# New constants for an order planner: engine durations by kind of instruction, and smaller margins between engines, in a gated mix of two attentions

## The chip, the cores and the metric

The kernel runs on one core of a Trainium2 chip. Its time is the device time of one execution in microseconds. The core's engines are TensorE (PE in the profile, with PEld for its weight loads), VectorE (DVE), ScalarE (ACT), GpSimd (POOL) and SyncE (SP, which issues DMAs here).

## The reference

Two attentions over the same x (2048 rows, 512 columns, bf16) are mixed by a gate per row. A is full attention with 32 heads of 16 columns; B looks at 8 positions back from each row, two apart.

```
g = sigmoid((x * gate_w).sum(-1))
A: q,k,v = split(x @ A_wqkv); p = softmax(q k^T / 4) over all 2048 keys; a = (p v) @ A_wo
B: q,k,v = split(x @ B_wqkv); keys and values at s, s-2, ..., s-14 (masked below 0);
   b = (softmax of 8 logits, times the 8 values) @ B_wo
out = g * a + (1 - g) * b
```

## The kernel before

**Attention A.** The work is cut into 32 periods, each one group of 4 heads and one block of 512 queries. A period has 64 units; a unit is one head, one tile of 128 keys and the 512 queries. For a unit PE computes scores into PSUM (a *ring fill*, tile `ring`), ACT takes the exponential into `pT`, and PE multiplies with the values into `acc` (`pvA`). Two ring buffers alternate, one of 3 units and one of 2, so ACT's instructions are 1536 and 1024 columns wide in turn, and a pair of them makes 5 units. Since ACT is not to do all of it, some groups of 4 units, called *quads*, are done on DVE: `conv` (`dt<-m_ps`, 128x512, four per quad) makes the bits of an approximate exponential by one multiply and add, `term` (`dt<-dt`, 128x2048, two per quad) makes two shifted copies, and PE sums the three with weighted values (`vd_all`). `start_quad` decides when a quad is begun, from the time that the planner sees left for the period and from what waits on DVE.

At the end of a period DVE transposes `acc` (`accT`), takes reciprocals (`rden`), POOL scales into `ott`, and DVE turns every second one back (`oat`), ready for the output product.

**Attention B.** It runs beside A, in 16 tiles of 128 rows (`b_tile`). PE projects, DVE evacuates into `kvs`, SP stores to a scratch in HBM and loads it again, shifted, as `ksh` and `vsh`. POOL then does all elementwise work of a tile in one chain: products with `ksh` (`prod<-ksh,qb`), tree sums (`prod<-prod`), logits `lg`, the subtraction of the maximum that DVE took (`mx`), after ACT's exponential and DVE's sum (`ssum`) the normalization, products with `vsh`, sums, and the result `obb`. PE transposes obb (`m_ps<-ident,obb`), DVE copies it to `obt`, and PE multiplies with `bwo`.

**Output.** `final` makes, for each 128 rows, the product with `bwo` (DVE evacuates it times 1-g into `fb`) and the product with A_wo (DVE evacuates it times g, plus fb, into `osb`); for the last block of queries the first three quarters of A's product are made ahead and kept as fp32 in `kt_all`.

**What sets the order.** All instructions are recorded first as `Op` objects, each with its engine, a duration in ns, dependencies, buffers to acquire and release, and a due time. The planner (`Sched`) then runs a model of the five engines in the build and writes the instructions out in the order of its start times; each engine executes its own list in that order, and semaphores keep the dependencies. So the durations in the planner are never executed. They decide which instruction is put ahead of which, and how many quads are given to DVE. The parts of the model that matter here are these:

- `est` gives the time at which an op is ready: the end of each dependency, plus the entry of `MARGIN` (line 58) for the pair of engines. An op that follows one on its own engine takes `gap` instead.
- `commit` advances an engine. DVE's `lock` ops and POOL's ops are made to exclude each other, with `HEAD` (line 66) as the part of an instruction that may overlap; `lead` (line 223) is how far the next instruction of an engine may start ahead of the end of the last.
- In `pe_source`, a ring fill is due 480 ns before the time at which ACT is expected to be idle, and line 1121 sums that up from the fills in hand. In `act_source`, line 1205, an exponential's duration is given. With ACT's lead of 127 ns a planned exponential takes 427 ns per unit and 83 ns.

```
act_idle = max(act_idle, f_["vis"]) + len(f_["us"]) * 427.0 + 83.0      # line 1121
op = Op("ACT", None, dur=nu * 426.7 + 210.0, name="exp")                # line 1205
```

- `warm` puts zero matmuls of the full array (`ones_t,zw`, 128x512) in front of an op while the planned share of streaming time in the last 3413 ns is under a threshold.

PE executes its list in order, so whatever PE waits for holds up the ring fills behind it.

Of the kernel before, what the change touches and what calls it, by code (L numbers as in the profile page):

```python
# [57 lines left out]
MARGIN = {("POOL", "DVE"): 2500.0, ("POOL", "PE"): 3000.0, ("DVE", "PE"): 300.0, ("PE", "DVE"): 100.0,  # L58
# [7 lines left out]
HEAD = {"DVE": 130.0, "POOL": 125.0}  # L66
# [51 lines left out]
class Sched:  # L118
# [82 lines left out]
    def commit(self, op, ready):  # L201
# [9 lines left out]
        else:  # L211
            op.start = max(self.t[e], ready)
            op.fin = op.start + op.dur
            if op.lock:
                begun, end = self.pool_op
                if begun <= op.start < end:
                    op.fin = max(op.fin, end - HEAD["DVE"] + op.dur)
                self.lock_end = op.fin
            elif e == "POOL":
                if op.start < self.lock_end:  # L220
                    op.fin = max(op.fin, self.lock_end - HEAD["POOL"] + op.dur)
                self.pool_op = (op.start, op.fin)
            lead = {"DVE": 80.0, "ACT": 127.0, "POOL": 40.0, "SP": 0.0}[e]
# [108 lines left out]
def kernel(  # L332
# [147 lines left out]
    load("x0", x_load(0), 6500.0)  # L480
    load("x1", x_load(1), 10000.0)
# [32 lines left out]
    S_.t["PE"] = 5600.0  # L514
# [5 lines left out]
    def k_proj(i, sc, due, first=False):  # L520
# [26 lines left out]
        p1 = Op("PE", part(0, 2), mms=COL4 * 3, deps=xt_ops[sc] + [ld["wk0" if i == 0 else "wk"]], due=due, acq=[hold], not_before=0.0 if first else due - 5000.0,  # L547
                name="k1")
        p2 = Op("PE", part(2, DC), mms=COL4 * 2, deps=[p1], due=due, name="k2")
        for o in (p1, p2):  # L550
            S_.add(o)
        if first:
            r = S_.add(Op("DVE", red, dur=700.0, deps=[p2], due=due, name="kred"))
            e = S_.add(Op("ACT", evac, dur=650.0, deps=[p2, r], due=due, rel=[hold], name="kev"))
        else:
            e = S_.add(Op("DVE", evac, dur=690.0, deps=[p2], allow=400.0, rel=[hold], name="kev"))
            r = S_.add(Op("DVE", red, dur=800.0, deps=[e], allow=1500.0, name="kred"))
# [5 lines left out]
    def selk(i, reds, due):  # L563
# [4 lines left out]
        selk_ops[i] = S_.add(Op("DVE", s, dur=650.0, deps=reds, due=due, name="selk"))  # L568
# [3 lines left out]
    def v_proj(h0, h1, tb, TB, due):  # L572
# [24 lines left out]
        ops.append(Op("DVE", evac, dur=690.0, allow=400.0, rel=[hold], name="vev"))  # L597
# [20 lines left out]
    def q_proj(c_, i, due):  # L618
# [24 lines left out]
        def evac():  # L643
# [6 lines left out]
               Op("DVE", absq, dur=690.0, allow=300.0, name="qabs"),  # L650
               Op("PE", bound, mms=COL4, due=due, rel=[ha], deps=[selk_ops[i]], name="qb"),
               Op("DVE", evac, dur=690.0, allow=300.0, rel=[hold], name="qev")]
# [46 lines left out]
    def b_tile(t, due):  # L699
# [19 lines left out]
        def store():  # L719
# [4 lines left out]
              Op("DVE", kev, dur=690.0, allow=600.0, rel=[hk], name="bkev")]  # L724
        vv = [Op("PE", pj("v", hv, 0, 2), mms=COL4 * 2, deps=xd + [kv[1]], due=due, acq=[hv], name="bv1"),
              Op("PE", pj("v", hv, 2, 4), mms=COL4 * 2, due=due, name="bv2"),
              Op("DVE", vev, dur=690.0, allow=600.0, deps=[kv[2]], rel=[hv], name="bvev")]
# [6 lines left out]
        def qev():  # L734
# [5 lines left out]
              Op("DVE", qev, dur=690.0, allow=1000.0, rel=[hq], name="bqev")]  # L740
# [35 lines left out]
        def padd(fn, dur, after_last=True, early=False, **kw):  # L776
            late = len(pool) > 17 and not early
            o = Op("POOL", fn, dur=dur, due=float(2 * t + (3 if late else 0)), name="bp", **kw)
            o.gap = 78.0 if after_last else -40.0
# [23 lines left out]
        for hf in range(2):  # L803
            for w_ in range(WH):
                first = w_ == 0
                padd(lmul(hf, w_), 1150.0, after_last=False, acq=([hp[hf]] if first else []) + ([hlg] if first and hf == 0 else []),
                     deps=[lk, qq[-1]] if first and hf == 0 else [])
            padd(ltree(hf, 8, 0, 2), 1255.0)
            padd(ltree(hf, 8, 2, 4), 1255.0, after_last=False)
            padd(ltree(hf, 4, 0, 4), 1255.0)  # L810
            padd(ltree(hf, 2, 0, 4), 612.0)
            padd(ltree(hf, 1, 0, 4), 418.0, rel=[hp[hf]] + ([hks, hqb] if hf else []))
# [32 lines left out]
        s_ = padd(sm_sub, 640.0, early=True, deps=[m_])  # L845
        x_ = S_.add(Op("ACT", sm_exp, dur=490.0, allow=500.0, deps=[s_], name="smexp"))
        d_ = S_.add(Op("DVE", sm_sum, dur=757.0, allow=2500.0, deps=[x_], name="smsum"))
        padd(sm_norm, 640.0, deps=[d_])
# [23 lines left out]
        level = []  # L872
        for w_ in range(W):
            padd(amul(w_, len(level)), 1095.0, after_last=w_ == 0, acq=[hp[2]] if w_ == 0 else [], deps=[lv] if w_ == 0 else [],
                 rel=[hvs, hlg] if w_ == W - 1 else [])
            level.append(0)
            while len(level) > 1 and level[-1] == level[-2] and len(level) + level[-1] < 5 and (level[-1] < 2):
                padd(aadd(len(level) - 2), 1255.0)
                level.pop()
                level[-1] += 1  # L880
        padd(fin1, 1264.0, acq=[hobb], rel=[hp[2]])
# [11 lines left out]
        def fin3():  # L893
# [4 lines left out]
             Op("DVE", fin3, dur=420.0, allow=800.0, rel=[hb], name="bf3")]  # L898
# [10 lines left out]
    def post(c_, i, pv_ops):  # L909
# [27 lines left out]
        def back():  # L937
# [3 lines left out]
        ops = [Op("DVE", turn, dur=720.0, allow=-2000.0, deps=pv_ops, acq=[hT],  # L941
                  rel=[acc_hold[(c_, i)]], name="accT", prompt=True),
               Op("DVE", rec, dur=240.0, allow=a, name="rec"),
               Op("DVE" if last else "POOL", scale, dur=450.0 if last else 640.0, due=-1.0, acq=[] if half else [ho], rel=[hT],
                  name="scale")]
        if half:
            ops.append(Op("DVE", back, dur=710.0, allow=a, acq=[oat_hold[pair]], rel=[ho], name="oatT"))
# [11 lines left out]
    def final(c_, tt, k0, k1, due):  # L959
# [31 lines left out]
        if not tail:  # L991
# [4 lines left out]
            fb = Op("DVE", bev, dur=690.0, allow=600.0, rel=[hold], deps=list(g_done), name="fbev")  # L996
# [15 lines left out]
        ops.append(Op("DVE", evac, dur=700.0, allow=0.0 if tail else 600.0, deps=[fb], rel=[hold] + ([] if tail else [hf]), name="fev"))  # L1012
# [92 lines left out]
    def pe_source(e):  # L1105
# [8 lines left out]
        if us and w < INF:  # L1114
# [3 lines left out]
            if r < INF and S_.slots["pTA" if n == 3 else "pTB"].when() < INF:  # L1118
                act_idle = S_.t["ACT"]
                for f_ in filled:  # L1120
                    act_idle = max(act_idle, f_["vis"]) + len(f_["us"]) * 427.0 + 83.0
# [74 lines left out]
    def act_source(e):  # L1196
# [8 lines left out]
        op = Op("ACT", None, dur=nu * 426.7 + 210.0, name="exp")  # L1205
# [101 lines left out]
    def make_quad(p, t, late):  # L1307
# [7 lines left out]
        for j in range(4):  # L1315
# [21 lines left out]
            a_ = S_.add(Op("DVE", conv, dur=690.0, deps=[f_] + aops[-1:], due=min(S_.now, late - 6000.0) + 300.0 * j - 5000.0, rel=[hold],  # L1337
# [137 lines left out]
```

## Time and profile before

| what | value |
|---|---|
| runs, us | 798.77, 799.01, 799.29, 801.13, 802.75; median 799.29 |
| the profiled execution, us | 801.13 |
| its span, first to last instruction, us | 798.8 |
| mean granted TensorE clock | 0.989 |
| ACT's exponentials (pT) | 656 instructions, 750.7 us busy |
| first pT starts, last one ends, us | 18.87, 788.3 |
| DVE's conversions dt<-m_ps and terms dt<-dt | 408, 269.8 us, and 204, 224.7 us |
| full-array zero matmuls into acc | 143, 50.2 us |
| POOL's first product, last obb ends, us | 56.41, 781.8 |

The profiled execution is one of the five runs. Busy time is the union of an engine's instructions; consecutive exponentials overlap a little, so their mean durations (1497 and 1072 ns for the two widths) add up to more than it. A row of the waits names who waited, for whom, the us in total, how often and the longest. In the timeline's rows stand start, length, engine, line, operation, count, and in brackets the idle time before and what ended it. Nearly all instructions carry line 382, that of the recording helper, so groups are told apart by their tiles.

### The profile page before, as it was taken

The page shows a single profiled execution, that of the slowest core. Times are in us where ns is not written, and L with a number is a line of the kernel's source. Part 1 is how long each engine was busy: PE and PEld are TensorE (multiplying, and loading weights), DVE is VectorE, ACT ScalarE, POOL GpSimd, SP SyncE. Part 2 cuts the span into 40 slices and gives each one's busy share as a digit, 9 for nine tenths or more (in the row PEclk, how much of TensorE's full clock was granted, in tenths as well). Part 3 has the DMA queues.
Part 4 walks back from the last instruction along what each step waited for, and adds up shares of the span by engine and source line. Part 5 has one row for each costly group of instructions (what it writes and reads, how often), then busy time and mean ns, then how long its engine had stood idle before and what let it go on. Part 6 is the DMA issues. An engine that isn't in the chain of part 4 may idle for free.

```text
span 798.8 us, 20306 instructions
## 1 busy us (share of the span) xinstructions
PE 743.6 (93%) x8523; PEld 234.6 (29%) x8523; DVE 679.7 (85%) x1019; ACT 756.9 (95%) x678; POOL 694.6 (87%) x599
## 2 busy tenths in 40 slices
PE   7999999999989999999999999999999999999996
PEld 2332233333222223332222222333322222322222
DVE  2569979888998998979988999898999998797886
ACT  2999999999999999998989999999999999999994
POOL 1028799999999999999989999999999999999991
PEclk9999999999999999999979999999999999999998
DMA  9220321122111211121012121120212212221100
GB/s 201 92 68 14 107 68 54 68 67 54 42 43 38 68 54 67 53 68 54 28 41 67 54 67 54 50 72 2 70 65 80 67 54 68 67 61 41 41 15 34
DMA packets 52074, 47.46 MB, mean 59 GB/s; under 512 B 12048, under 2 KB 49424, under 8 KB 51984
## 3 DMA queue, kind: packets, MB, share of 16 engines
q1 hardware_dynamic: 50400, 45.98, 18.5%
q8 instruction: 66, 1.08, 0.5%
q10 hardware_dynamic: 1584, 0.20, 0.2%
q14 instruction: 24, 0.20, 0.1%
HBM read 37.75 MB, written 6.32 MB: 55 GB/s over the span
## 4 chain that ended last, share of the span: by engine, by line
ACT 39%; PE 26%; DVE 19%; issue 11%; POOL 2%; SPq 1%; DMA 1%; ACTq 0%; DVEq 0%; POOLq 0%
ACT pT L382 39%; DVE dt L382 13%; PE m_ps L382 10%; PE acc L382 9%; PE ring L382 6%; POOL prod L382 2%; SPq L382 1%; DVE accT L382 1%; DVE kt_all L382 1%; DVE absq L382 1%; ACT lg L382 1%; DVE kmax_all L382 1%; DMA xT<-in_A_x_dram 0%; DVE kvs L382 0%; DVE selk_all L382 0%
## 5 line engine op out<-in xcount | busy, mean ns | idle before, releaser
L382 ACT ACTIVATE pT<-ring 128x1536 bf16<-128x1536 f32 (+1 forms) x656 | 750.7, 1284 | 17.6 <-PE ring L382 16.1
L382 PE MATMUL ring<-qt,kt_all 32*128 32x512 bf16 x1640 | 279.0, 384 | 28.7 <-ACT pT L382 25.7
L382 DVE TENSOR_SCALAR dt<-m_ps 128x512 uint16<-128x512 f32 x408 | 269.8, 679 | 42.0 <-PE m_ps L382 33.5
L382 POOL TENSOR_TENSOR prod<-prod 128x512 f32<-128x512 f32 x224 | 294.2, 1319 | 10.7
L382 DVE TENSOR_SCALAR dt<-dt 128x2048 uint16<-128x2048 uint16 x204 | 224.7, 1103 | 1.1 <-PE acc L382 0.4
L382 PEld LDWEIGHTS <-kt_all 32*128 32x128 bf16 (+1 forms) x2304 | 92.1, 91 | 289.6 <-issue 279.1
L382 POOL TENSOR_TENSOR prod<-ksh,qb 128x512 f32<-128x512 bf16 x128 | 160.8, 1284 | 12.5 <-DVE qb L382 5.3
L382 PE MATMUL acc<-pT,vp_all 128*17 128x512 bf16 x1640 | 159.5, 385 | 0.1
L382 POOL TENSOR_TENSOR prod<-vsh,lg 128x512 f32<-128x512 bf16 x128 | 151.7, 1201 | 4.7
L382 PE MATMUL m_ps<-qt,kt_all 32*128 32x512 bf16 x408 | 138.7, 385 | 7.3 <-DVE dt L382 4.5
L382 PEld LDWEIGHTS <-vp_all 128*17 128x17 bf16 x2048 | 47.2, 88 | 109.0 <-issue 100.0
L382 POOL TENSOR_TENSOR ott<-accT,rden 128x256 bf16<-128x256 f32 x31 | 24.5, 790 | 54.1 <-DVE rden L382 54.1
L382 PE MATMUL acc<-ones_t,zw 128*128 128x512 bf16 (+1 forms) x271 | 62.9, 392 | 3.7 <-DVE accT L382 3.7
L382 PE MATMUL acc<-dt,vd_all 128*17 128x512 bf16 x816 | 62.1, 381 | 0.0
L382 PE MATMUL m_ps<-bw,xT 128*32 128x512 bf16 x768 | 55.9, 382 | 1.2 <-DVE kt_all L382 0.4
L382 PEld LDWEIGHTS <-xT 128*32 128x32 bf16 (+1 forms) x1152 | 32.5, 96 | 28.9 <-issue 22.1
L382 PE MATMUL acc<-dt,vp_all 128*17 128x512 bf16 x408 | 40.2, 384 | 0.0
L382 PE MATMUL m_ps<-xT,wkv 128*16 128x512 bf16 x512 | 38.1, 387 | 1.3 <-DMA xT<-in_A_x_dram 1.3
L382 PE MATMUL m_ps<-xT,wq 128*16 128x512 bf16 x496 | 36.4, 380 | 0.0
L382 PEld LDWEIGHTS <-zw 128*32 128x32 bf16 (+1 forms) x401 | 19.4, 94 | 54.6 <-issue 51.2
L382 DVE CAST kvs<-m_ps 128x512 bf16<-128x512 f32 x32 | 21.8, 681 | 9.7 <-PE m_ps L382 9.5
L382 DVE CAST kt_all<-m_ps 128x512 bf16<-128x512 f32 x28 | 19.2, 684 | 11.6 <-PE m_ps L382 11.5
(71 smaller groups left out, 451.0 us busy)
## 6 DMA issues: line engine op xcount, KB each, us to landing
ksh<-kv_scr SPq DMA_DIRECT2D x16, 1024.0 KB, 5.7
vsh<-kv_scr SPq DMA_DIRECT2D x16, 1024.0 KB, 5.4
kv_scr<-kvs SPq DMA_DIRECT2D x16, 256.0 KB, 2.0
out_dram<-osb SPq DMA_DIRECT2D x16, 128.0 KB, 1.7
bw<-in_B_wqkv_dram SPq DMA_DIRECT2D x1, 1536.0 KB, 10.3
wkv<-in_A_wqkv_dram SPq DMA_DIRECT2D x2, 448.0 KB, 5.1
bwo<-in_B_wo_dram SPq DMA_DIRECT2D x1, 512.0 KB, 4.5
woarr<-in_A_wo_dram SPq DMA_DIRECT2D x8, 64.0 KB, 2.3
```

The lines of the kernel that those rows point to most:

```text
L382: return chain_on(key, f(*a, **k))
```

## The change

Only constants of the planner change, and flags that say which op follows its predecessor's result.

- **ACT**: the fixed part of an exponential goes from 210 to 178 (83 to 51 after the lead), in both places.
- **Margins**: POOL to DVE 2500 to 1500, POOL to PE 3000 to 1500, DVE to PE 300 to 200, PE to DVE 100 to 60.
- **POOL**: durations of single ops by some ns (products 1150 to 1149 and 1095 to 1094, tree sums 1255 to 1260, sums 1255 to 1268, `sm_sub` and `sm_norm` 640 to 628, `scale` 640 to 616), the gap after an independent op from -40 to -43, and `after_last` set by what each op really depends on.
- **DVE**: evacuations and conversions 690 to 683, `kred` 800 to 677, `selk` 650 to 446 and now among the lock ops, `fbev` and `fev` 690 and 700 to 745, `smsum` 757 to 791, transposes 720 to 716 and 710 to 707.
- **Lock**: HEAD 130 and 125 to 133 and 137, leads of DVE and POOL 80 and 40 to 83 and 43.
- **Start**: PE's first planned time 5600 to 7800, the landing of x 6500 and 10000 to 8100 and 11500, and the first K projection counted twice as long.

In the order that is built, ACT has 1644 units in 658 instructions where it had 1640 in 656, DVE 101 quads where it had 102, and PE 111 full-array zero matmuls where it had 145. SP issues the same transfers, some in another order.

```
-MARGIN = {("POOL", "DVE"): 2500.0, ("POOL", "PE"): 3000.0, ("DVE", "PE"): 300.0, ("PE", "DVE"): 100.0,
+MARGIN = {("POOL", "DVE"): 1500.0, ("POOL", "PE"): 1500.0, ("DVE", "PE"): 200.0, ("PE", "DVE"): 60.0,
-HEAD = {"DVE": 130.0, "POOL": 125.0}
+HEAD = {"DVE": 133.0, "POOL": 137.0}
...
-                    op.fin = max(op.fin, end - HEAD["DVE"] + op.dur)
+                    op.fin = max(op.fin, end - HEAD["DVE"] + (op.dur if op.name != "selk" else 254.0))
-            lead = {"DVE": 80.0, "ACT": 127.0, "POOL": 40.0, "SP": 0.0}[e]
+            lead = {"DVE": 83.0, "ACT": 127.0, "POOL": 43.0, "SP": 0.0}[e]
...
-    load("x0", x_load(0), 6500.0)
-    load("x1", x_load(1), 10000.0)
+    load("x0", x_load(0), 8100.0)
+    load("x1", x_load(1), 11500.0)
-    S_.t["PE"] = 5600.0
+    S_.t["PE"] = 7800.0
...
+        slow = 2 if first and sc == 0 else 1
-        p1 = Op("PE", part(0, 2), mms=COL4 * 3, deps=xt_ops[sc] + [ld["wk0" if i == 0 else "wk"]], due=due, acq=[hold], not_before=0.0 if first else due - 5000.0,
+        p1 = Op("PE", part(0, 2), mms=COL4 * (3 * slow), deps=xt_ops[sc] + [ld["wk0" if i == 0 else "wk"]], due=due, acq=[hold], not_before=0.0 if first else due - 5000.0,
-            e = S_.add(Op("DVE", evac, dur=690.0, deps=[p2], allow=400.0, rel=[hold], name="kev"))
-            r = S_.add(Op("DVE", red, dur=800.0, deps=[e], allow=1500.0, name="kred"))
+            e = S_.add(Op("DVE", evac, dur=683.0, deps=[p2], allow=400.0, rel=[hold], name="kev"))
+            r = S_.add(Op("DVE", red, dur=677.0, deps=[e], allow=1500.0, name="kred"))
-        selk_ops[i] = S_.add(Op("DVE", s, dur=650.0, deps=reds, due=due, name="selk"))
+        selk_ops[i] = S_.add(Op("DVE", s, dur=446.0, deps=reds, due=due, lock=True, name="selk"))
...
-            o.gap = 78.0 if after_last else -40.0
+            o.gap = 78.0 if after_last else -43.0
-                padd(lmul(hf, w_), 1150.0, after_last=False, acq=([hp[hf]] if first else []) + ([hlg] if first and hf == 0 else []),
+                padd(lmul(hf, w_), 1149.0, after_last=first, acq=([hp[hf]] if first else []) + ([hlg] if first and hf == 0 else []),
-            padd(ltree(hf, 8, 0, 2), 1255.0)
-            padd(ltree(hf, 8, 2, 4), 1255.0, after_last=False)
+            padd(ltree(hf, 8, 0, 2), 1260.0, after_last=False)
+            padd(ltree(hf, 8, 2, 4), 1260.0, after_last=False)
-        s_ = padd(sm_sub, 640.0, early=True, deps=[m_])
+        s_ = padd(sm_sub, 628.0, after_last=False, early=True, deps=[m_])
-            padd(amul(w_, len(level)), 1095.0, after_last=w_ == 0, acq=[hp[2]] if w_ == 0 else [], deps=[lv] if w_ == 0 else [],
+            padd(amul(w_, len(level)), 1094.0, after_last=added or w_ == 0, acq=[hp[2]] if w_ == 0 else [], deps=[lv] if w_ == 0 else [],
...
-                    act_idle = max(act_idle, f_["vis"]) + len(f_["us"]) * 427.0 + 83.0
+                    act_idle = max(act_idle, f_["vis"]) + len(f_["us"]) * 427.0 + 51.0
-        op = Op("ACT", None, dur=nu * 426.7 + 210.0, name="exp")
+        op = Op("ACT", None, dur=nu * 426.7 + 178.0, name="exp")
```

## The prediction

> **What bounds the kernel now.** I read the page's busy shares first, then the clock by slice, then ACT's rows in the timeline, then the waits and the tail.
>
> ```profile
> PE 743.6 (93%) x8523; PEld 234.6 (29%) x8523; DVE 679.7 (85%) x1019; ACT 756.9 (95%) x678; POOL 694.6 (87%) x599
> PEclk9999999999999999999979999999999999999998
> ```
>
> Four engines are over 80% busy, so no share names the bound. ACT is the first suspect: 95%, nearly all of it the pT exponentials. These run from 18.87 us to 769.03 + 19.27 = 788.3 us, that is 769.4 us; ahead lie 18.9 us of loading and first projections, behind 10.5 us of output. Next, what an undisturbed pair (one of 3 units, one of 2) takes.
>
> ```profile
> 428.91 4.62 ACT L382 ACTIVATE pT<-ring 128x1536 bf16<-128x1536 f32 x4
> 433.39 0.44 ACT L382 ACTIVATE lg<-lg 128x256 f32<-128x256 f32 x1
> 433.70 29.62 ACT L382 ACTIVATE pT<-ring 128x1536 bf16<-128x1536 f32 x26
> ...
> 464.07 15.18 ACT L382 ACTIVATE pT<-ring 128x1536 bf16<-128x1536 f32 x13 [0.76 <-PE ring L382]
> ```
>
> Four exponentials start at 428.91 and the next operation at 433.39: 4.48 us for two pairs, **2.24 us a pair**, 0.448 us a unit. The lg exponential adds 433.70 - 433.39 = 0.31 us. The 1640 units are 328 pairs: 328 x 2.24 + 16 x 0.31 + 0.2 for the gate's own = 739.9 us. So 769.4 - 739.9 = **29.5 us are stalls of ACT**. The idle column shows only part (16.1 below), since consecutive exponentials overlap and a short delay leaves no gap. The last row shows their form: ACT waits for a ring fill by PE.
>
> ```profile
> POOL ott L382 <- DVE rden L382: 54.1, 6, 47.7
> DVE dt L382 <- PE m_ps L382: 33.5, 61, 1.6
> PE ring L382 <- ACT pT L382: 25.7, 86, 0.7
> ACT pT L382 <- PE ring L382: 16.1, 24, 2.0
> ```
>
> Columns: us in total, times, longest. PE and ACT wait for each other in turn; neither has a lead.
>
> Two of the stalls are clock dips. In the windows 399 to 413 us (clock 0.63) and 599 to 606 us (0.76) ACT is busy 10.44 of 14 and 5.18 of 7: 3.6 + 1.8 = 5.4 us. The other 24.1 us are spread out: 73 ns a pair. The planner of before prices a pair at 5 x 426.7 + 2 x 83 = 2299 ns, 60 ns over the measured 2240. It places PE's and DVE's work for an ACT that is slower than the real one; the real one waits where the others come at the planned pace. 328 x 60 ns = **19.7 us** of the 24.1 have this explanation.
>
> POOL runs almost without a gap. Its first product starts at 56.41 and its last obb ends at 780.17 + 1.60 = 781.8 us, 725.4 us, with 12.5 us idle (ott 2.6 and 2.4, qb 5.3, the rest small).
>
> **The Trainium skill.** Three places bear.
> - "ScalarE: Activation LUTs", Rules for kernel authors, states some 0.3 us per ACTIVATE and 0.83 ns per element. The slope agrees: means of 1497 and 1072 ns for 1536 and 1024 columns, 0.83 ns per column. The fixed part does not show in the step, because the operations overlap; the trace's 2.24 is used.
> - "SBUF — State Buffer", Who interferes with whom: a DVE operation in a two-port mode and a POOL operation exclude each other for a whole instruction. The trace agrees: the DVE terms dt<-dt take 623 ns at least and 1103 in the mean, and POOL's prod<-prod of 128x512 1403 against a median of 1271.
> - "TensorE: Matmul & The Clock Gate", What's actually happening: an idle PE falls to half its clock. The two dips are the trace's cases. The full-array zero matmuls are the kernel's remedy.
>
> **The change, part by part.** No operand shape and no buffer changes; constants of the planner do, and with them the order.
> 1. *ACT's price, 83 to 51 ns per instruction.* A planned pair becomes 5 x 426.7 + 2 x 51 = 2236 ns, the measured 2240. The pacing explained above goes: at most -19.7 us.
> 2. *One quad less on DVE* (102 to 101 in the built order; dt<-m_ps 408 to 404, dt<-dt 204 to 202). Its four units go to ACT: + 4 x 0.448 = **+1.8 us** on the path. DVE gains 4 x 0.679 + 2 x 1.103 = 4.9 us, off the path.
> 3. *Zero matmuls of the full array, 145 to 111.* Acc's 143 are 50.2 us of busy time, 0.35 each: 34 x 0.35 = 11.9 us less on PE. What ACT waits for is PE, so this is the part of the 19.7 that I can count on.
> 4. *Margins cut* (POOL to DVE 2500 to 1500 ns, POOL to PE 3000 to 1500, DVE to PE 300 to 200, PE to DVE 100 to 60). New waits can arise where real work is later than planned. Behind a waiting DVE mx stand the quads' conversions; behind a waiting PE instruction stand the ring fills, then ACT. Before shows no wait of DVE's mx or ssum for POOL. PE waits for DVE 39 times, 19 us with the start and the tail; in some 30 ordinary ones I allow the margin's 100 ns each: **+3 us**. The lower bound for all margins is below nothing, since earlier work can shorten other waits (-3, as much again). The upper is 32 waits for POOL (one mx, one transposition per tile) of 1.0 and 1.5 us, 40 us.
> 5. *POOL's, DVE's and selk's durations, selk under the lock, begin of the first loads and of PE.* Up to the first pair of ring fills PE's order is the same (272 rows), so the 18.87 us stay. After it V projections come ahead of K projections; DVE has gaps there (3.07 and 1.28 us before kt_all), which cover them. I take nothing; without the cover one projection's evacuation, 0.7 us, is exposed. POOL's first product stands after unit 75 instead of 80: 5 x 0.448 = 2.2 us earlier.
> 6. *DMAs.* SP issues the same transfers; a few stores, loads and outputs swap places. A ksh load lands in 5.7 us (median), and POOL waited for one only, 4.8 us, at the start. Nothing, as the other tile's buffer covers it; one load without it would cost up to 5.7.
> 7. *The tail.* The last transposition of obb stood after ring unit 1635 of 1640; now it stands behind all 1644, with bwo, fb, kt_all, one output pass and its store after it. From the rows of before: 0.40 + 0.41 + 1.04 + 0.75 + 0.71 + 0.40 + 0.75, then 2.7 from osb's end to the span's, and some 1.0 of handovers: 8.2 us from POOL's end to the end.
>
> Sum for ACT: between 11.9 and 19.7 us gained, the middle 15.8; less 1.8 and less 3.0: **-11.0 us**. Span 798.8 - 11.0 = 787.8. The profiled execution took 801.13 us, 2.3 outside the span; so 790.1 for such a one. The median of the runs shown is 799.29, 1.84 below it: 799.29 - 11.0 = **788.3**, given as 788.
>
> Check by POOL's chain: end 781.8 - 2.2 = 779.6 with the same idle time, + 8.2 = 787.8. Both chains end together, so more from ACT alone would not show. If POOL lost 7 of its 12.5 us idle, it would allow a span of 781.
>
> **Rivals.**
> - *(a) POOL holds back a part.* For: after 90 us POOL is never idle for more than 2.4 us at a time, and its last tile now ends the kernel. If its start is not earlier and two of its feeds come late as qb did (5.3), less half of that overlapped: 788 + 2.2 + 5.3 / 2 = 793. Against: qb of tile 1 is now placed earlier, after unit 135 and not 145.
> - *(b) The clock.* With 34 zero matmuls fewer, PE may fall under the activity that keeps its clock. Two dips cost 5.4 us; four more of their size give 10.8 and cancel the gain: 799. Against: the planner holds the same threshold, and a faster ACT brings more real work per us.
> - *(c) Slower: the margins.* The 32 waits for POOL take the place of the ring waits. At 0.7 us each on the path, 22.4 us on top of 788.3: 811. It decides from 11.0 / 32 = 0.35 us each. For: DVE's terms and POOL lock each other out, and their length is the least predictable in the trace. Against: in before POOL starts each subtraction of mx within some 5 units of its place in the order.
> - *(d) The planner's ACT price does not pace anything*, the 73 ns a pair are mere collisions: then only +1.8 and +3 remain, 804. Against: PE spends 25.7 us waiting for ACT, so ACT does set the pace in places.
>
> **How the numbers follow.** Main case 0.54 (780 to 792 by itself), (a) 0.22, (b) 0.08, (c) 0.10, (d) 0.06. About 0.3%, 2.4 us, is what a measurement of this kernel can tell from no change. Faster takes the main case and (a), and a little of (b): 0.78. Same is most of (b): 0.07. Slower is (c) and (d): 0.15. Low end 780, where POOL's chain allows no more; high end 802, which leaves out (c), (d)'s end, and the gains below 780: about 0.2.
>
> **What would show it.** Right: pairs still at 2.24, 1644 units, ACT's stalls down from 29.5 to about 17 us, fewer and shorter ring waits, and POOL's obb ending some 8 us before the end. Step 4 wrong: DVE mx or PE m_ps waiting for POOL with more than a few us. Step 3 wrong: slices with PEclk below 9 beyond two. Step 1 wrong: ring waits as before although PE does less. The forecast is wrong if ACT's stretch is longer than 765 us.

## The result and the profile after

The changed kernel takes 800.28 us (median of 43 runs, 794.96 to 806.46), the kernel before 801.46 (median of 80 runs, 798.5 to 810.23). The ratio is **0.9977, 95% interval 0.9961 to 0.9992**: 1.8 us less by the ratio, 1.2 between the medians, inside the 0.3% that the prediction called no change. 788 was forecast. The profiled execution took 800.33 us, with a span of 798.3 (before 801.13 and 798.8). Ratios, here and below, leave out executions more than 1.5% above the fastest of their kernel.

Even this much is a matter of the clock. A run's time follows its mean granted clock (worked out at the end), and the changed kernel's runs had a mean clock of 0.989, those of before, run beside the experiments below, 0.982 to 0.985 (five sets, 226 runs). Straight lines of time against clock through these runs give 799.7 us for before at a clock of 0.989 (799.5 to 799.9 in the five sets) and 800.1 for the changed kernel, with some 0.4 us of uncertainty. **At one clock nothing is gained.** Whether the new order brings the higher clock, or the occasion did, is not shown; the prediction counted on no such gain.

From the page: busy us and share by engine, and the clock by slice.

```profile
PE 741.8 (93%) x8481; PEld 238.4 (30%) x8481; DVE 672.6 (84%) x1013; ACT 755.9 (95%) x680; POOL 695.4 (87%) x599
PEclk9999999999999989999999999999999999999998
```

PE's busy time fell by 1.8 us in all. The full-array zero matmuls into `acc` did go from 143 and 50.2 us to 107 and 38.2, the 12 us that were priced; but busy time is a union of pipelined matmuls with modelled ends, and most of the 12 us was filled by others. The shares are those of before.

From the waits: us in total, times, longest.

```profile
POOL ott L382 <- DVE rden L382: 57.9, 12, 49.7
PE ring L382 <- ACT pT L382: 29.0, 88, 1.0
DVE dt L382 <- PE m_ps L382: 17.3, 40, 1.1
ACT pT L382 <- PE ring L382: 13.7, 19, 1.8
POOL lg L382 <- DVE mx L382: 6.6, 6, 2.2
POOL lg L382 <- DVE rr L382: 5.8, 2, 4.9
```

ACT's idle waits for PE fell from 16.1 to 13.7 us only, PE's for ACT rose from 25.7 to 29.0, DVE's conversions wait half as long (17.3 us, 33.5 before). POOL waits for DVE's `mx` six times (once before).

The gaps hide part of ACT's stalls. So here, and for every kernel below, I took each step from one ACT instruction's start to the next and subtracted the shortest step that the trace shows for that width: 1331 ns for 1536 columns, 904 for 1024, 306 for 256. What is left is stall; a step that starts within 2 us of a stretch of half clock (a *dip*) is counted apart, the rest is called **ordinary**. This gives 31.1 us for before (29.5 in the prediction, whose pair was 5 ns longer), 24.5 of it ordinary. Three of the ordinary figures below (27.3, 43.6 and 30.3) hold one stall of 4.4 to 5.4 us each that starts ahead of a dip and runs into it; they would be that much lower if it were counted with the dip.

| profiled execution | before | after | difference |
|---|---|---|---|
| ACT's units | 1640 | 1644 | + 4 x 0.448 = +1.8 us |
| ordinary stalls, us | 24.5 | 19.5 | -5.0 |
| stalls in clock dips, us | 6.6 | 5.7 | -0.9 |
| last exponential ends, us | 788.3 | 784.3 | -4.0 |
| from there to the end (tail), us | 10.5 | 13.9 | +3.4 |

So ACT did get 4.0 us shorter, and the tail gave 3.4 back. The worst stretch that is left, ACT's rows in the timeline (start, length, count; in brackets the idle time before, and what ended it):

```profile
146.33 1.45 ACT L382 ACTIVATE pT<-ring 128x1536 bf16<-128x1536 f32 x1 [0.76 <-PE ring L382]
148.27 2.37 ACT L382 ACTIVATE pT<-ring 128x1024 bf16<-128x1024 f32 x2 [0.49 <-PE ring L382]
151.54 3.44 ACT L382 ACTIVATE pT<-ring 128x1024 bf16<-128x1024 f32 x3 [0.91 <-PE ring L382]
156.30 3.71 ACT L382 ACTIVATE pT<-ring 128x1536 bf16<-128x1536 f32 x3 [1.32 <-PE ring L382]
```

PE's rows ahead of the last of these:

```profile
153.75 1.04 PE L382 MATMUL m_ps<-xT,wkv 128*16 128x512 bf16 x16
154.62 1.04 PE L382 MATMUL m_ps<-bw,xT 128*32 128x512 bf16 x16
155.48 0.39 PE L382 MATMUL acc<-pT,vp_all 128*17 128x512 bf16 x4
155.80 0.39 PE L382 MATMUL ring<-qt,kt_all 32*128 32x512 bf16 x3
```

Ahead of the fill for 156.30 (at 155.80), PE executed 16 `m_ps<-xT,wkv`, 16 `m_ps<-bw,xT` and 4 `pvA` in one piece and never waited. This is the usual form: of the 17.2 us of ordinary stalls over 30 ns, 12.2 came while PE worked without a pause between the freeing of the ring buffer and its fill, 5.0 while PE itself waited. In before the two parts are 12.9 and 9.4 us: the stalls behind a block of other work hardly changed, those in which PE waited fell by 4.4.

The tail, from the timeline:

```profile
763.28 21.04 ACT L382 ACTIVATE pT<-ring 128x1024 bf16<-128x1024 f32 x19
...
788.59 1.27 POOL L382 TENSOR_TENSOR obb<-prod 128x512 bf16<-128x512 f32 x1
...
790.03 0.62 PE L382 MATMUL m_ps<-ident,obb 128*32 128x128 bf16 x16 [0.28 <-DVE osb L382]
...
791.17 1.90 PE L382 MATMUL m_ps<-bwo,obt 128*32 128x512 bf16 x16
...
794.85 0.75 DVE L382 SCALAR_TENSOR_TENSOR osb<-m_ps,gate,kt_all 128x512 bf16<-128x512 f32 x1
```

POOL's last obb ends at 789.9, 8.1 us later than before, and from there 8.4 us pass to the end. The clock dipped within this tail, at 790.0 and at 796.8: the 16 matmuls of `bwo` at 791.17 took 1.90 us, 16 such ones in before's tail 1.04.

### The profile page after: what moved, and what is told of

Same layout as the page of the kernel before. It is cut to its first block, busy times and chain, and to the rows that moved or that the text cites. A ratio compares the mean times of both kernels' runs of the same rounds, so it can differ in the third digit from the quotient of the medians.

```text
span 798.3 us, 20219 instructions
## 1 busy us (share of the span) xinstructions
PE 741.8 (93%) x8481; PEld 238.4 (30%) x8481; DVE 672.6 (84%) x1013; ACT 755.9 (95%) x680; POOL 695.4 (87%) x599
## 4 chain that ended last, share of the span: by engine, by line
ACT 32%; PE 28%; POOL 15%; DVE 13%; issue 10%; SPq 1%; DMA 0%; POOLq 0%; DVEq 0%; ACTq 0%
ACT pT L382 31%; POOL prod L382 13%; PE m_ps L382 13%; DVE dt L382 9%; PE acc L382 8%; PE ring L382 7%; SPq L382 1%; POOL lg L382 1%; POOL obb L382 1%; DVE accT L382 0%; POOL ott L382 0%; DVE kt_all L382 0%; DMA xT<-in_A_x_dram 0%; DVE vd_all L382 0%; DVE osb L382 0%
## 5 line engine op out<-in xcount | busy, mean ns | idle before, releaser
L382 ACT ACTIVATE pT<-ring 128x1536 bf16<-128x1536 f32 (+1 forms) x658 | 749.6, 1316 | 14.4 <-PE ring L382 13.7
L382 POOL TENSOR_TENSOR prod<-prod 128x512 f32<-128x512 f32 x224 | 295.6, 1326 | 10.8
L382 DVE TENSOR_SCALAR dt<-m_ps 128x512 uint16<-128x512 f32 x404 | 266.1, 677 | 29.9 <-PE m_ps L382 17.3
L382 DVE TENSOR_SCALAR dt<-dt 128x2048 uint16<-128x2048 uint16 x202 | 219.8, 1093 | 2.5 <-PE acc L382 1.8
L382 PEld LDWEIGHTS <-kt_all 32*128 32x128 bf16 (+1 forms) x2304 | 98.9, 92 | 296.1 <-issue 283.6
L382 PE MATMUL m_ps<-qt,kt_all 32*128 32x512 bf16 x404 | 136.3, 383 | 4.8 <-DVE dt L382 3.3
L382 PE MATMUL acc<-ones_t,zw 128*32 128x512 bf16 (+1 forms) x235 | 51.2, 392 | 1.3 <-DVE accT L382 1.2
L382 PEld LDWEIGHTS <-xT 128*32 128x32 bf16 (+1 forms) x1152 | 31.8, 96 | 33.4 <-issue 27.1
L382 DVE TENSOR_SCALAR absq<-m_ps 128x512 int32<-128x512 int32 x31 | 21.3, 687 | 15.6 <-PE m_ps L382 15.3
L382 PEld LDWEIGHTS <-zw 128*32 128x32 bf16 (+1 forms) x367 | 16.8, 95 | 41.3 <-issue 39.6
```

Source lines behind the costliest of these rows:

```text
L382: return chain_on(key, f(*a, **k))
```

## The experiments

All ratios are to the kernel before, run beside each kernel on the same chip, with 95% intervals. Units, quads and zero matmuls are those of the built order. Stalls and tails are from one profiled execution each. A time "at 0.989" is read from the straight line of time against clock through a kernel's runs, as above; it takes out what differs by the clock alone.

### Parts undone, and parts alone

**Margins undone**: the changed kernel with the margins of before.

```
-MARGIN = {("POOL", "DVE"): 1500.0, ("POOL", "PE"): 1500.0, ("DVE", "PE"): 200.0, ("PE", "DVE"): 60.0,
+MARGIN = {("POOL", "DVE"): 2500.0, ("POOL", "PE"): 3000.0, ("DVE", "PE"): 300.0, ("PE", "DVE"): 100.0,
```

> The changed kernel with the four margins of before (2500, 3000, 300, 100); every duration as in the changed kernel. Theory P (POOL's waits for DVE's mx and rr come from mx and ssum being placed at their dues, not from the margins): POOL's last obb still ends at 780-790 us, ratio to before 0.993-1.003. Theory M (the smaller margins cause the new waits): POOL's waits for mx and rr fall from 12 us to under 2 us, POOL ends about 8 us earlier, ratio 0.985-0.990.

Measured 1.0089 [1.0063, 1.0115], above what either theory allowed. The smaller margins did not cost; without them the change is slower.

**ACT's price alone**: before with this edit.

```
-... * 427.0 + 83.0        -... nu * 426.7 + 210.0
+... * 427.0 + 51.0        +... nu * 426.7 + 178.0
```

> The kernel before with ACT's two constants alone changed (83 to 51 and 210 to 178). The order then has 1656 units for ACT and 98 quads. If ACT's price paces the work as the forecast had it, ACT's stalls fall from 29.5 us by 10 us or more while 16 more units cost 7.2 us: ACT ends near 784 us and the ratio to before is 0.990-0.996. If the price paces nothing, 7 us longer: ratio 1.005-1.010.

Measured 1.0101 [1.005, 1.0151]: the part that was to bring everything is a loss by itself. Its order has 1656 units and 98 quads.

**All but ACT's price**: the changed kernel with 83 and 210.

> The changed kernel with ACT's two constants put back (83 and 210). The order has 1624 units for ACT and 106 quads: 20 units fewer than the changed kernel, 16 fewer than before. Theory U (ACT's time follows its units, 0.448 us each, and the planner's ACT price gains nothing itself but costs quads; margins and durations gave the gain): 20 x 0.448 = 9 us less than the changed kernel, ratio to before 0.984-0.991. Theory P (the price paces the engines, margins give nothing): slower than the changed kernel, ratio 1.000-1.012.

Measured 0.9937 [0.991, 0.9964], 1624 units, 106 quads: faster than the changed kernel, but by less than theory U's 9 us. By the ratio this is the fastest kernel here that leaves nothing out; a part of it is clock (798.5 us at 0.989, where before has 799.7).

**Margins alone, durations alone**: before with the four new margins; and the changed kernel with the margins and ACT's price of before.

> The kernel before with the four smaller margins alone. ACT has 1628 units, DVE 105 quads, PE 119 zero matmuls in the built order. Theory Q (the change acts through the number of units that the planner leaves to ACT): 12 units fewer are 12 x 0.448 = 5.4 us, ratio 0.993. Step 4 of the prediction (smaller margins make new waits, +3 us and up to +40): 1.00 to 1.01 although ACT has less to do. Theory R (an order is luck, of some 0.5 per cent either way): anything from 0.99 to 1.01, with the ordinary stalls of ACT taking up or adding to the 5.4 us.

> The changed kernel with the margins and the price of ACT of the kernel before, so durations, dependency flags and the start alone. 1632 units, 104 quads, 137 zero matmuls. Theory Q: 8 units fewer are 3.6 us, ratio 0.9955. The prediction took nothing for this part: 1.000. If margins and durations add up, this one times the margins alone gives the 0.994 of the two together.

Measured 0.9993 [0.997, 1.0015] and 1.0084 [1.0058, 1.0111]. They don't add up: 0.9993 x 1.0084 = 1.0077, and together they give 0.9937. Theory Q failed for both: 12 units fewer without a gain, and 8 units fewer but slower.

| kernel | units / quads | ordinary stalls, us | tail, us | ratio | us at 0.989 |
|---|---|---|---|---|---|
| before | 1640 / 102 | 24.5 | 10.5 | 1 | 799.7 |
| price | 1656 / 98 | 21.0 | 14.9 | 1.0101 | 809.4 |
| margins | 1628 / 105 | 26.2 | 14.4 | 0.9993 | 797.8 |
| durations | 1632 / 104 | 33.4 | 13.0 | 1.0084 | 807.3 |
| price, durations | 1652 / 99 | 28.4 | 11.4 | 1.0089 | 810.3 |
| margins, durations | 1624 / 106 | 25.8 | 13.6 | 0.9937 | 798.5 |
| all (after) | 1644 / 101 | 19.5 | 13.9 | 0.9977 | 800.1 |

The last column is uncertain by 0.2 to 1.0 us (two standard errors).

Read in pairs, the lower price takes 3.5, 5.0 and 6.3 us off the ordinary stalls (rows 1 and 2, 4 and 5, 6 and 7), and each time puts 16 or 20 units, 7.2 or 9.0 us, on ACT. No pair gets faster: 1.0101, 1.0089 / 1.0084 = 1.0005, 0.9977 / 0.9937 = 1.0040; at one clock 9.7, 3.0 and 1.6 us slower. The smaller margins (rows 1 and 3, 4 and 6, 5 and 7) take 12, 8 and 8 units off ACT; ordinary stalls go 1.7 us up in the first pair and 7.6 and 8.9 us down in the others; the times are 0.9993, 0.9854 and 0.9889, at one clock 1.9, 8.8 and 10.2 us less.

### Does the price act through the quads?

QUAD, in `start_quad`, limits when a quad may still be begun. More quads again, once without and once with the lower price: the kernel with all but the price, and the one with the price alone, each with

```
-    QUAD = 6000.0
+    QUAD = 4000.0
```

> As the run before, with QUAD, the time that a new quad is taken to need, cut from 6000 to 4000 ns: 1616 units and 108 quads. Theory U: 8 units fewer, 3.6 us less than all-but-price, ratio 0.980-0.988, unless DVE is full: then ACT's stalls grow by more than 3.6 us and the ratio is 0.988-0.996.

> The kernel before with ACT's price alone, and QUAD 4000 instead of 6000: 1648 units and 100 quads, 8 units fewer than with the price alone (ratio 1.010 there). Theory U: 3.6 us less than that, ratio 1.003-1.008, as 8 units more than before cost 0.45%. Theory P (at nearly equal units the price must show its gain of 10 us or more): ratio under 0.997.

Measured 1.0005 [0.9982, 1.0028] with 1616 units, where 1624 gave 0.9937, outside of all that was expected; and 1.0068 [1.0042, 1.0093] with 1648, where 1656 gave 1.0101, as theory U has it. Fewer units are no sure gain by themselves: ordinary stalls were 29.0 and 27.3 us (25.8 and 21.0 at 6000).

**Price at equal quads**: the price alone with QUAD at 2000.

> The kernel before with ACT's price of 51 and 178 and the limit for beginning a quad at 2000 instead of 6000, which gives 1640 units and 102 quads, as many as in the kernel before; 139 zero matmuls (145). Theory Q (the price acts through the number of quads alone): within 0.3 per cent of before. Step 1 of the prediction (the price paces the engines): ordinary stalls down from 24 us by 12 to 20, ratio 0.976 to 0.985. Theory R (luck of the order): up to 1 per cent either way, with ordinary stalls or the tail to match.

Measured 1.0239 [1.0206, 1.0272], outside of all three theories. The trace shows why, and that this was no fair test. PE's rows at the end of a period, then ACT's:

```profile
123.10 0.39 PE L382 MATMUL ring<-qt,kt_all 32*128 32x512 bf16 x2
123.65 0.59 PE L382 MATMUL acc<-ones_t,zw 128*128 128x512 bf16 x2 [0.16 <-issue]
124.23 0.37 PE L382 MATMUL m_ps<-qt,kt_all 32*128 32x512 bf16 x1
...
126.58 1.04 PE L382 MATMUL m_ps<-xT,wkv 128*16 128x512 bf16 x16
...
128.08 0.60 PE L382 MATMUL acc<-dt,vd_all 128*17 128x512 bf16 x8
...
129.82 0.40 PE L382 MATMUL acc<-ones_t,zw 128*32 128x512 bf16 x4 [0.25 <-DVE accT L382]
...
130.37 0.39 PE L382 MATMUL ring<-qt,kt_all 32*128 32x512 bf16 x3
```

```profile
131.14 3.71 ACT L382 ACTIVATE pT<-ring 128x1536 bf16<-128x1536 f32 x3 [5.83 <-PE ring L382]
```

Between the fills at 123.10 and 130.37 PE makes none: it works on a late quad (`m_ps<-qt`, `acc<-dt`), whose sums must be done before `acc` can change to the next period, and pads the time with zero matmuls. ACT stands 5.83 us. Two such places cost 6.2 and 4.8 us, and the ordinary stalls are 43.6 in all. At such a place a quad that is begun too late costs more than the 1.8 us of the four units that it saves.

From the other side, with the price of before: QUAD at 14000, which gives the 1656 units and 98 quads of the price alone, and QUAD at 10000, which gives the 1640 and 102 of before in another order.

> The kernel before with the limit for beginning a quad at 10000 instead of 6000 and nothing else: 1640 units and 102 quads as before, 141 zero matmuls (145), but another order of the same work; no duration, price or margin of the planner is corrected. Theory R (any new order moves the time by some 0.5 per cent or more either way, through collisions on PE): a ratio away from 1 by 0.3 per cent or more, with ACT's ordinary stalls away from 24.5 us to match. Theory Q (units decide): within 0.3 per cent of before.

> The kernel before with the limit for beginning a quad at 14000, which gives 1656 units and 98 quads, as many as the kernel with ACT's price of 51 alone (ratio 1.010), but with the price of before. Theory Q (the price acts through the quads that the planner drops): 16 units are 7.2 us, ratio 1.009 to 1.011. If the lower price costs or gives something of its own at equal quads, the two kernels differ: pacing (step 1) would put this one 12 us above the other, 1.025; theory R (luck of the order) up to 0.5 per cent on either side of 1.009.

Measured 0.9982 [0.9952, 1.0013] for the reordered one and **1.0104 [1.006, 1.0147]** for the one with fewer quads. The price alone gave 1.0101. So with 98 quads the kernel is 1% slower with the new price and without it. The two intervals leave room for some 5 us between them, either way, but not for the 11.9 to 19.7 us that step 1 gave to pacing. At 0.989 the price alone has 809.4 us and fewer quads 805.3, each uncertain by 1.1: in this reading the price costs some 4 us besides its quads. It gains in neither.

The ordinary stalls of these executions are best read per us of ACT's stretch outside of dips, since the one with fewer quads ran for 60 us at half clock: before has 33 ns in a us, fewer quads 31, the price alone 28, the reordered kernel 29 (21.4 us).

The reordered kernel, with nothing corrected and no count of units or quads changed, cannot be told from before in time. That speaks against theory R, though it is one order, and its interval reaches to -0.5%. Its ordinary stalls did fall, by as much as the price took off them, and of those over 30 ns 12.3 us came behind a block and 5.6 while PE waited, nearly as in the changed kernel. So 3 us less of them in one profiled execution is no sign that a correction worked.

### Does ACT, PE or POOL set the time by itself?

**Lighter POOL**: 96 of the changed kernel's sums over half the columns (the other half is left out).

```
-                G.tensor_tensor(out=prod[:, k, :], in0=prod[:, k, :], in1=prod[:, k + 1, :], op=ALU.add)
+                G.tensor_tensor(out=prod[:, k, 0:256], in0=prod[:, k, 0:256], in1=prod[:, k + 1, 0:256], op=ALU.add)
```

> The changed kernel with its order untouched, but POOL's 96 sums of attended values (aadd, six per tile) add only 256 of the 512 columns; half of the columns of B's result lack their sums. POOL has some 96 x 0.6 = 58 us less to do; ACT, DVE and PE have the same lists. Theory P (POOL's chain of 713 us, starting at 54.8 us, has become the end of the kernel, because it is 9 us longer idle than before): POOL stops mattering, the last obb ends before ACT does, ACT ends at about 784 us or some us earlier, and the span falls from 798.3 to 788-795, a ratio to before of 0.985-0.995. Theory A (ACT's and PE's stalls and the clock set the end, POOL's late end is a symptom): within 2 us of the changed kernel, ratio 0.996-0.999.

Measured 0.9982 [0.9953, 1.0012], the same as after. Page and waits:

```profile
PE 735.5 (92%) x8437; PEld 236.4 (29%) x8481; DVE 664.6 (83%) x1013; ACT 757.2 (94%) x680; POOL 634.5 (79%) x599
...
POOL ott L382 <- DVE rden L382: 106.2, 27, 49.7
POOL lg L382 <- DVE mx L382: 19.2, 10, 6.4
```

POOL has 60.9 us less to do, and waits for DVE instead, 48.3 us more for `rden` and 12.6 for `mx`. Its last obb ends at 790.8, now 0.4 us ahead of ACT's last exponential (in the changed kernel 5.5 behind it; this execution lost 8.3 us more of ACT's time in dips). The time did not fall, 800.3 us at 0.989: theory A. POOL is not the bound.

**No zero matmuls**: the changed kernel with both thresholds of `warm` at -1.

```
-STREAM = 0.48
-LEAST = 0.42
+STREAM = -1.0
+LEAST = -1.0
```

> The changed kernel with no zero matmuls of the full array at all (thresholds below zero): 111 x 0.35 = 39 us less for PE, 1636 units. Theory L (what ACT waits for is PE's load, as in step 3 of the forecast): ACT's ordinary stalls fall from 19.5 to under 12 us, ratio 0.985-0.990 where the clock holds. Theory C (collisions of single blocks with a fill, not load): ordinary stalls stay at 17-20 us. The clock: if the zeros are what keeps it, the dips' share rises from 6 us to over 20 and the ratio is over 1.01.

Measured 1.0384 [1.0329, 1.0439]. The clock by slice and the ring wait:

```profile
PEclk9987999998699899699999999999989969999898
...
ACT pT L382 <- PE ring L382: 34.2, 44, 3.4
```

111 x 0.35 = 39 us less work for PE, and the ordinary stalls are 16.3 us, 3.2 below after. But they come from less time: outside of dips ACT's stretch has 623 us here and 750 in after, so it is 26 ns of stall in a us both times. Another 37.2 us are lost in stretches of half clock. Freed PE time did not come to ACT: theory C.

**Lighter ACT**: the changed kernel with 105 exponentials over 448 columns of 512; the order of every engine stays.

```
-            A.activation(out=pT[:, 0:nu, :], in_=f_["ring"][:, 0:nu, :], func=ACT.Exp, scale=float(DH) ** -0.5)
+            nx[0] += nu == 3
+            f_["wd"] = wd = QW - 64 if nu == 3 and nx[0] > 12 and nx[0] % 3 == 0 else QW
+            A.activation(out=pT[:, 0:nu, 0:wd], in_=f_["ring"][:, 0:nu, 0:wd], func=ACT.Exp, scale=float(DH) ** -0.5)
...
-            emit_pv_mm(p, t, j, grp["pT"][:, s_, :], cnt[p][j] == 0)
+            x_ = grp["pT"][:, s_, 0:256]
+            if grp["wd"] < QW:
+                x_ = _ap(x_, [list(x_.ap[0]), [192, 2], [1, 256]])
+            else:
+                x_ = grp["pT"][:, s_, :]
+            emit_pv_mm(p, t, j, x_, cnt[p][j] == 0)
```

> The changed kernel with every third exponential of 3 units from the twelfth on taken over 448 of 512 columns (105 instructions, 3 x 64 columns fewer each at 0.833 ns: 16.8 us less work for ACT); PE reads some columns twice instead, so its work and every engine's order stay. What is left out: one eighth of the exponentials in those instructions. Theory A (ACT's stretch sets the time, the others only interrupt it): 12 to 17 us less, ratio 0.977 to 0.983. Theory I (ACT, PE and DVE hold each other in the written order, so that ACT alone is no bound): under 8 us, ratio 0.988 or more, and ACT's stalls up by the rest.

Measured 0.9913 [0.9883, 0.9943]; to the changed kernel 0.9913 / 0.9977 = 0.9936, 5.1 us of the 16.8 taken away. Page and waits:

```profile
PE 730.0 (92%) x8437; PEld 233.5 (29%) x8481; DVE 673.2 (85%) x1013; ACT 742.6 (93%) x680; POOL 695.0 (87%) x599
...
PE ring L382 <- ACT pT L382: 26.9, 81, 0.8
ACT pT L382 <- PE ring L382: 21.4, 31, 2.7
```

ACT now waits 21.4 us for fills, 7.7 more than in after, and its ordinary stalls rise from 19.5 to 24.8. In this execution dips took another 7.6 us more. Theory I is the nearer one: of a us taken off ACT about 0.3 reach the end (6.1 of 16.8 us at 0.989). Of the rest, some 5 us came back as waits for PE; how much the dips owe to the edit is not shown.

### Other orders

Four tries at a faster version, and what they were to tell: DVE's `mx` and `ssum` urgent in the changed kernel (`allow` 2000 and 2500 to 0); B begun earlier (22000 to 12000 in `b_tile`'s due time); more zero matmuls (thresholds 0.48 and 0.42 to 0.53 and 0.47); fills due 80 ns earlier (480 to 560). The last kernel has all but ACT's price, the earlier B and more zero matmuls.

> The changed kernel with the dues of DVE's smmax and smsum moved forward (allowances 2000 and 2500 to 0), so that POOL's inputs from DVE stand ahead of conversions in DVE's order; 99 quads, 1652 units. Theory P: POOL's waits for mx and rr (6.6 + 5.8 us) mostly go, POOL's last obb ends 5-10 us earlier, the end follows until ACT (8 units more, 3.6 us) takes over: ratio to before 0.988-0.996. Theory A: the 8 units make it longer, ratio 1.000-1.004.

> The changed kernel with the first tile of B due 12 us instead of 22 us after the first fill: POOL's first product stands after unit 63 instead of 75, the last obb after 1600 of 1636 units instead of 1615 of 1644; 103 quads. Theory T (the changed kernel's tail is 13.9 us long, against 10.5 before, because the last tile of B finishes behind ACT's last exponential): the tail falls to 10-11.5 us, and 8 units fewer give 3.6 us: 5-7 us less than the changed kernel, ratio 0.989-0.992. Theory N (the tail's length is that of the last period's own chain): tail 13-14.5 us, only the units count, ratio 0.992-0.995.

> The changed kernel with the thresholds of the planned streaming share raised by 0.05 (0.53 and 0.47): 152 zero matmuls of the full array instead of 111, 1640 units. Theory D (dips of PE's clock cost 5.3 us per hundredth of mean clock, and PE's load costs nothing): the mean clock over the runs rises from 0.989 to 0.994 or more, at full clock the time stays within 3 us of the changed kernel, ratio 0.990-0.996. Theory L (PE's load is what ACT waits for): 41 x 0.35 = 14 us more for PE lengthen the ordinary stalls by 5 us or more, ratio 1.000-1.010.

> The changed kernel with a ring fill due 560 instead of 480 ns before ACT is idle; 1644 units as there, 109 zero matmuls. Theory C (the ordinary stalls are single collisions: a fill planned with hardly any slack behind a block of other PE work, 50-300 ns each): the ordinary stalls, 19.5 us, fall by a third or more, to 8-13 us, and the number of stalls over 30 ns from 79 to under 50; ratio 0.985-0.992. Theory S (they come from work that waits for another engine, or from blocks that no due time moves): stalls 17-22 us, ratio 0.996-1.001.

> All but ACT's price, with B 10 us earlier and the raised thresholds: 1628 units, 178 zero matmuls, first product after unit 58. If units, tail and clock add: 16 units fewer than the changed kernel -7.2, tail -2 to -3, clock -3 to -5, ordinary stalls as in the run with all but the price (+6): ratio 0.982-0.990. If POOL's earlier start or the zeros cost something on PE: 0.992-1.000.

| kernel | units | ordinary stalls, us | tail, us | ratio |
|---|---|---|---|---|
| `mx`, `ssum` urgent | 1652 | 21.2 | 12.1 | 1.0034 [0.9997, 1.0072] |
| B earlier | 1636 | 30.3 | 13.2 | 1.0163 [1.0123, 1.0204] |
| more zero matmuls | 1640 | 25.8 | 15.3 | 1.0076 [1.0055, 1.0098] |
| fills 80 ns earlier | 1644 | 19.3 | 14.3 | 1.0056 [1.0032, 1.008] |
| three together | 1628 | 31.7 | 11.6 | 0.9989 [0.9952, 1.0027] |

None gains on the changed kernel. Theory A held for the first, L for more zero matmuls, and the last fell in its slower range; for the other two neither theory gave the ratio. The earlier B adds 10.8 us of ordinary stalls to those of after; more zero matmuls 6.3. For the fills due 80 ns earlier the terms of the profiled executions are nearly those of after, and still its ratio is 0.8%, 6.3 us, above; some 4 of these are clock (a mean of 0.981 over its runs, 0.989 over after's, at 5.3 us for 0.01, see the end), the other 2 stay open. The edits move counts and collisions together, by a per cent either way, and their working had priced one of the two.

## Why the prediction was wrong

**Step 1 failed**, and with it the forecast. The price of ACT was read as the pace at which the planner runs PE and DVE, worth 19.7 us. The numbers under it were right (a pair takes 2240 ns, 2299 were planned). But the price also decides how long a period lasts in the model, and with it how many quads DVE gets there: with a faster ACT, 98 instead of 102. The kernel with those 16 units more is 1.0% slower, and 98 quads without the new price are as slow by the ratio. The ordinary stalls of kernels that differ by the price differ by 3.5 to 6.3 us, where the sum had 11.9 to 19.7; a reordering alone moved them by some 3, and they did not outweigh the units in any of three pairs. Rival (d), that the stalls are mere collisions, was nearest: most ordinary stalls come while PE executes a block of other matmuls (12.2 us of 17.2, as much as in before). Its chance was 0.06, and its 804 us were too many.

**Step 2** had the right number for the whole change (+4 units, 1.8 us) and hid two opposite ones: +20 by the price, and -16 by margins and durations together. Costing the net count kept me from seeing that the parts work against each other.

**Step 3**, "the part that I can count on", failed. PE's shorter list did not come to ACT: with 39 us of zero matmuls gone, ACT's ordinary stalls stayed at 26 ns in a us. What stands ahead of a fill counts more than what PE has to do in all; in the other direction, 41 more zero matmuls came with 6.3 us more of them.

**Step 4 had the wrong sign.** The +3 us were longer waits of PE for DVE; these fell, from 39 waits and 19.1 us to 30 and 15.7. The upper end of 40 was new waits for POOL; the trace after shows none of DVE's `mx`, and half a us of PE's weight load for obb. In none of three pairs did smaller margins cost. They made the change 1.1% faster (1.0089 without, 0.9977 with); in the terms that is 8.9 us of ordinary stalls and 8 units, 3.6 us, less 2.5 of a longer tail. By themselves they gave next to nothing (0.9993).

**Step 5** took nothing for the durations; alone they cost 0.84%, with 8.9 us more ordinary stalls. With the new margins they give 0.6% by the ratio, and nothing at one clock (798.5 us, 797.8 without them). So what they cost depends on what they are combined with; why they cost by themselves stays open. POOL's first product came at 54.8 (54.2 forecast), and the 18.9 us to the first exponential stayed.

**Step 6** holds: POOL's waits for ksh are 2.8 us.

**Step 7** was right on the piece that it priced (8.4 us from POOL's end to the end, 8.2 forecast) and wrong on where that piece begins. "With the same idle time" POOL was to end at 779.6; it ended at 789.9, since its waits after the first product grew from 12.7 to 22.3 us (the prediction's sum had 12.5 for before). It is not shown that the late obb makes the longer tail. PE's transposition of it (790.03) waited last for DVE's `osb`, a dip lengthened what came after, and other kernels have such tails without a late obb: with the price alone it ended 7.7 us ahead of ACT's last exponential, and the tail is 14.9 us. With the lighter POOL it ended 0.4 us ahead, for a tail of 12.2 and no gain in time. What sets the tail in each order stays open.

**The form of the sum failed too.** It was made along ACT, as though a us saved there were a us at the end. The lighter ACT gives 0.3. ACT, PE, DVE and POOL execute written lists that hold each other; ACT's 95% is how full such a list is, not a sign that it alone is the bound.

The order of the parts then: +1.8 units, -5.0 and -0.9 stalls, +3.4 tail, together -0.7 us for a span that fell by 0.5. Over the runs, at one clock, it is 799.7 and 800.1 us. That the time came out so near to before's is not what any step gave: gains and losses of some us each happened to cancel, and the 0.23% that was measured fits the higher clock of the changed kernel's runs.

## What to carry to other kernels

A number in a planner acts on every decision that reads it or the times made from it; `start_quad` does not read ACT's price, and still gave fewer quads. Before pricing a corrected cost, list those decisions, and count what each part of the change does to the division of work by itself; the count of the whole hides parts that cancel. Where four engines are over 80% busy, take work away from one with the order kept, before trusting a sum along it: here POOL's was worth nothing, ACT's a third. Where runs list their clock, compare at one clock. And where work is shared between a fast and a slow path, a share that is begun too late at a boundary can cost more (5.83 us at one place) than the work it saves.

## What the runs showed of the hardware

- **The clock between runs.** Over the runs of one kernel the time follows the mean granted clock: straight lines through the runs give about 5.3 us for each 0.01 (before 4.9 to 5.7 in five sets of runs, after 5.7). At 800 us a mean lower by 0.01 is 16 us of half clock, so a us at half clock costs some 0.33 us, less than the half that PE itself loses.
- **Dips follow stretches in which PE has less to do.** The Trainium skill, "TensorE: Matmul & The Clock Gate", What's actually happening, has recent activity release the throttle. The traces agree in direction, with PE far from idle. The dips last 3.4 us or a few times that. Leaving out the tail, in the 3.4 us ahead of before's two dips PE was busy for 2.61 and 2.43 us, ahead of the one in after for 1.75; its mean share is 93%. Without zero matmuls there are 15 dips ahead of the tail, and PE was busy for 1.84 to 2.75 of the 3.4 us ahead of 14 of them (the other followed a full stretch). It is no threshold: in before PE was busy for 2.39 of the 3.4 us from 217.4 on, with no dip after them.
- **The full-array zero matmuls kept the clock, up to a point.** Without them PE was 91% busy and its mean clock 0.922 over the runs; with 111 of them it was 93% and 0.989; with 152 it was 0.989 again. The share over the whole span does not tell this; the short stretches do.
- **The fixed part of an exponential** shows in the steps as (1331 - 904) / 512 = 0.834 ns per column and 904 - 1024 x 0.834 = 50 ns, the 51 of the corrected price. The correction was true; it was what the planner did with it that cost.
